# Output projection of an attention kernel: full-height products in one score bank, or pairs of 64-row products in the two banks of a pair

## The chip, the cores and the metric

One core of a Trainium2 chip runs the whole kernel. The metric is device time in microseconds (us) of one execution; lower is better. The granted TensorE clock was 0.999 of full speed over the profiled execution.

## The reference, cut to what matters

Two attentions over the same input are computed and mixed by a gate. `A` has 32 heads of 16, causal inside four blocks of 512 tokens, with a memory carried from block to block; `B` is a full attention over 2048 tokens. Each has its own output projection, and the change is in these two products and their sum.

```python
def _A_ref(x, wq, wk, wv, wo, beta):
    ...
    logits = jnp.einsum("bhqd,bhkd->bhqk", qs, ks) * scale + mask
    p = _softmax(logits, axis=-1)
    a_dot = jnp.einsum("bhqk,bhkd->bhqd", p, vs)
    ...
    o = g * a_mem + (1.0 - g) * a_dot
    ...
    return o @ wo

def _B_ref(x, wqkv, wo):
    ...
    o = jnp.einsum("bhqk,bhkd->bhqd", p, v)
    return (lambda x, *d: x.transpose(*d))(o, 0, 2, 1, 3).reshape(B, S, D) @ wo

g = _sigmoid((x * gate_w).sum(-1, keepdims=True))
return g * a + (1 - g) * b
```

The kernel puts the gate into the attention outputs, so that an output tile of 128 tokens is `oA @ woA + oB @ woB`, each with 512 inner elements and 512 columns.

## The kernel before, in words

**Units.** The attention is cut into 64 units: 32 of `A` (numbers 0 to 31) and 32 of `B` (32 to 63). A unit is four heads by 512 queries. After a stage of projections, the main loop runs `k` from 0 to 31 and does unit `32 + k` of `B` and unit `k` of `A` in 37 *groups*, numbered `n`. The instructions stand in the program in the order in which this loop writes them; nothing reorders them.

**A group** of `B` (`n` below 32) has, in this order:
- `t_group` (matmuls L528, exponentials on ScalarE L534): the transposed scores of two heads, as two products of 64 rows, one on the upper and one on the lower half of TensorE's rows. Each writes a bank of its own, out of the three banks `tb0`, `tb1` and `mb` (`misc` and `bank` hand out the one used longest ago). In the texts below this pair is T, with the group's number: T1 is that of group 1.
- the tasks that `plan` has for the group: nearly always one `s_b` (matmuls L474, reduction on VectorE L476), a pair of 64-row products for a later unit. It writes the two banks of one *pair of score banks*, `SBK[0]` or `SBK[1]` (`sbk` in the profile), handed out in turn by `rot`; VectorE then takes the row maxima over both banks. This pair is S below, and its reduction R.
- `pvs`: the products of exponentials and values (L550), four heads side by side in one bank, `pvb`. These are PV below. Group 1 has none.

The last five groups do the same for the `A` unit, with `s_a` (L452, L456, reductions L460 and L462) in place of `s_b`. `fin_copy` (L557) brings `pvb` out once per unit; the copy of the `A` unit falls into group 0 of the next `k`.

**The output slots.** From `k = 9` on, when four column blocks of heads are finished, one *slot* per `k` computes half of an output tile: slot `k - 9`, in group 1, by `out_mm(c, t, a)`. With `a = 0` it is the `A` half, with `a = 1` the `B` half of the same tile. `extras` puts it into `pre[1]`, behind the `s_b` of that group. The operands are split in a high and a low part: `AT["oh"]`, `AT["ol"]` hold the attention output of 128 tokens (made by `out_split` at the end of the unit before, on ScalarE L609 and GpSimd L610), `AT["wh"]`, `AT["wl"]` the weights. `TERMS` names three products (high by high, high by low, low by high), each over four blocks of 128 inner rows, so a slot is 12 products of 128 rows by 512 columns (L616), added up in one bank of the three. For `a = 0` ScalarE copies the bank to `yo` (L620); for `a = 1` VectorE adds it to `yo` (L623), and the SP queue sends the tile out (L624). At `k = 31` there is a second slot in group 28; what is left of the projection is done behind the loop.

VectorE, ScalarE and GpSimd each work through their instructions in program order, and so does the SP queue, which issues the transfers.

Of the kernel before, what the change touches and what calls it, by code (L numbers as in the profile page):

```python
# [7 lines left out]
FT = mybir.dt.float32  # L8
# [3 lines left out]
AF = mybir.ActivationFunctionType  # L12
OP = mybir.AluOpType
# [7 lines left out]
DM = 512  # L21
# [13 lines left out]
def gated_mix_kernel(ctx, tc, xt, wq, wk, wv, wo, beta, wqkv, wob, gate_w, out):  # L35
    nc = tc.nc
    outr = out.rearrange("b s d -> (b s) d")
# [47 lines left out]
    SBK = [PS.tile([128, 2, C], FT, name=f"sbk{i}") for i in range(2)]  # L85
# [23 lines left out]
    def rot(key, lst):  # L109
        i = cnt.get(key, 0)  # L110
        cnt[key] = i + 1
        return lst[i % len(lst)]
# [165 lines left out]
    TERMS = ((0, 0), (0, 1), (1, 0))  # L278
# [127 lines left out]
    def load_q(u):  # L406
        kd, qd, c = UN[u]
        load_qk(q_of(u), kd, 0, qd, c)

    def load_ka(u):  # L410
        kd, qd, c = UN[u]
        load_qk(KA[u % 2], kd, 1, qd, c)
# [67 lines left out]
    def m_chain(k):  # L480
        mx = pair_max(k)
        if k == 1:
            nc.vector.memset(mx[:, 0], 0.0)
        if k < 32:
            nc.vector.tensor_reduce(mx[:, 1], MXB.pop(32 + k).rearrange("q j p i c -> q (j p) i c"), axis=AX.X,
                                    op=OP.max)
        else:
            nc.vector.memset(mx[:, 1], 0.0)
        del MX[k]
        mx = mx.rearrange("q u h i -> q (u h i)")  # L490
        m8 = M8[k] = W.tile([128, 2, 32], FT, name="m8")
        hi = W.tile([128, 32], FR, name="mhi")
        nc.vector.tensor_scalar(hi, mx, -1.0, None, op0=OP.mult)
        nc.vector.tensor_copy(m8[:, 0], hi)
        nc.vector.scalar_tensor_tensor(m8[:, 1], mx, -1.0, hi, op0=OP.mult, op1=OP.subtract)
# [16 lines left out]
    AT = {}  # L512
# [3 lines left out]
    def t_group(u, n, banks):  # L516


        kd, qd, c = UN[u]
        bs = [bank(banks) for _ in range(2)]  # L520
        c0 = 0
        for it, hs in (((n // 2, (n % 2 * 2, n % 2 * 2 + 1)),) if kd == "B" else GA[n]):
            q0 = 128 * it if kd == "A" else 0
            w = C - q0
            pn = it if kd == "B" else it % 2
            for j, h in enumerate(hs):
                r = slice(64 * j, 64 * j + 64)
                nc.tensor.matmul(bs[j][:, c0:c0 + w], k_of(u, h // 2)[r, 128 * it:128 * it + 128],  # L528
                                 q_of(u)[r, h // 2, q0:], start=True, stop=True)
                PT[u, it, h] = PTILE[pn % 2][:, 2 + j if (kd, it) == ("A", 2) else h][:, c0:c0 + w]  # L530
            c0 += w
        for j in range(2):
            pt = PTILE[pn % 2][:, 2 + j if (kd, n) == ("A", 4) else hs[j]]
            nc.scalar.activation(pt, bs[j], AF.Exp, scale=SCALE)  # L534
            if kd == "A":
                m = pt[:, :128] if n < 2 else pt.rearrange("p (a t) -> p a t", a=4)[:, ::3 if n < 4 else 2]
                nc.gpsimd.affine_select(out=m, in_=m, pattern=[[1, 128]] if n < 2 else [[0, 2], [1, 128]],  # L537
                                        compare_op=OP.is_ge, fill=0.0, base=0, channel_multiplier=-1)
# [73 lines left out]
    def out_mm(c, t, a):  # L612
# [8 lines left out]
        else:  # L621
            tt = 4 * c + t
            nc.vector.tensor_tensor(AT["yo"], b, AT["yo"], op=OP.add)  # L623
            nc.sync.dma_start(outr[tt * 128:(tt + 1) * 128, :], AT["yo"])  # L624

    def tail_ops(t):
        s = KB[2 * (t // 2)][:, t % 2]
        return [s[:, 1024 * n:1024 * n + 1024].rearrange("p (g a t) -> p g a t", g=4, a=2) for n in range(2)]
# [29 lines left out]
    def todo(fn, *a):  # L658
        return lambda: fn(*a)
# [90 lines left out]
    for blk in range(16):  # L750
        g, c = divmod(blk, 4)
# [8 lines left out]
        n = blk + 1 + (c == 2)  # L760
# [74 lines left out]
    def late():  # L835
        proj.close()
        L = AT["L"] = ctx.enter_context(tc.tile_pool(name="late", bufs=1))
        VB[1] = L.tile([128, NT, 8, E + 1], FT, name="vb1")
        AT["o"] = [L.tile([128, 4, 2, C], FT, name=f"o{n}") for n in range(2)]
        AT["wh"] = L.tile([128, 4, 2, DM], FR, name="wh")  # L840
        AT["wl"] = L.tile([128, 4, 2, DM], FR, name="wl")
        AT["d"] = [L.tile([128, C], FT, name=f"d{n}") for n in range(2)]
        AT["oh"] = L.tile([128, 4, 2, 128], FR, name="oh")
        AT["ol"] = L.tile([128, 4, 2, 128], FR, name="ol")
        for p in range(2):
            set_aux(KB[2][:, p], 0)
# [6 lines left out]
    def pvs(k, n):  # L853

        ua, ub = k, 32 + k
        if n == 0:
            if k:
                pv(ua - 1, 2)
                fin_copy(ua - 1)
        elif k == 31 and n < 2 * NT:  # L860
            if n % 2 and n > 1:
                pv(ub, n // 2 - 1)
        elif 2 <= n < 2 * NT + 2:
            pv(ub, n // 2 - 1, n % 2 * 256, n % 2 * 256 + 256)
            if n == 2 * NT + 1:
                fin_copy(ub)
        elif n > 2 * NT + 1:
            m = n - 2 * NT - 2
            if m < 2:
                pv(ua, 0, 256 * m, 256 * m + 256)  # L870
            else:
                pv(ua, 1)
                pv(ua, 3)

    def extras(k):

        pre, post = {}, {}
        if not k:
            for n in range(4):
                pre[2 * n] = [fill[n - 4]]  # L880
        post[2 * S_LAST + 4] = [todo(m_rows, k + 1)]
        for n, at in [(k - 9, 1)] + [(23, 2 * OMI)] * (k == 31):
            if n >= 0:
                pre[at] = [todo(out_mm, n // 8, n // 2 % 4, n % 2)]
        return pre, post

    def beside(k, it):

        for f, it0, u in ((fin_load, NT + 1, 32 + k), (fin_rec, 5, 31 + k), (fin_bc, 6, 31 + k),
                          (fin_load, 1, k - 1), (fin_rec, 6, k - 1), (fin_bc, S_LAST + 2, k - 1)):  # L890
            if it == it0 and (k or it0 > NT):
                f(u)
        c, j = divmod(k - 1, 8)
        if k and j % 2:
            for kd, it0 in (("B", 9), ("A", 13)):
                if it == it0:
                    fin_norm(kd, j // 2, c)
        if k >= 8 and k % 2 == 0 and it == NT + 2:
            out_split(k // 8 - 1, k // 2 % 4)
        if (k, it) == (31, 4):  # L900
            grest = AT["grest"] = AT["o"][0][64:, 0, 0]
            nc.sync.dma_start(grest, GD[3 * C:].rearrange("(o t) -> o t", o=1).to_broadcast([64, C]))
        if (k, it) == (31, 9):
            grest = AT["grest"]
            nc.vector.tensor_scalar(grest, grest, nh[64:, 3:4], None, op0=OP.mult)
        if (k, it) == (31, NT + 2):
            fin_rec(63)
        if k == 31 and it == 13:
            o = AT["o"][1][:64, 3, 0]
            nc.gpsimd.tensor_tensor(o, o, AT["d"][0][:64], op=OP.mult)  # L910
        if k == 31 and it < 8 and it % 2 == 0:
            for a in range(2):
                tail_split(it // 2, slice(0, 3), a)


    ex = [extras(k) for k in range(32)]
    plan = {}

# [13 lines left out]
    for k in range(32):  # L932
        ua, ub = k, 32 + k
        banks = T3 + [b[:, 0] for b in SBK] * (k == 31)
        for n in range(NG):
            it = n // 2 if n < NG - 1 else NT + 2
            t_group(*(ub, n) if n < 2 * NT else (ua, n - 2 * NT), banks)
            for f in plan.get((k, n), []) + ex[k][0].get(n, []):
                f()
            pvs(k, n)  # L940
            for f in ex[k][1].get(n, []):
                f()
            if n % 2 == 0 and n < NG - 1:
                continue
            beside(k, it)
            if it == S_LAST:
                m_chain(k + 1)
            if it == 4 and not k:
                late()
            if it == 4 and not k:  # L950
                load_q(ub + 2)
                for c in range(NC4):
                    load_kb(2, c)
            if it == NT and k < 29:
                load_q(ub + 3)
                load_kb(k + 3)
            if it == 6 and k < 31:
                load_q(ua + 1)
                load_ka(ua + 1)
                if (ua + 1) % 2 == 0:  # L960
                    load_va(ua + 1)
            if it == 9:
                if k % 2 == 0 and k < 30:
                    load_vb(k // 2 + 1)
                if 1 <= k <= 4:
                    load_wo(k - 1)
# [55 lines left out]
```

## Time and profile before

| | |
|---|---|
| Median of 3 runs | 1960.63 us (1957.93 to 1960.81) |
| Profiled execution, its own time | 1956.4 us |
| Span, first to last instruction | 1954.7 us |
| Busy TensorE, VectorE, ScalarE, GpSimd | 1930.3, 1629.9, 1433.4, 275.8 us |
| Output slots in the loop | 24, each 12 matmuls of L616 |

A busy TensorE is counted from the start of a matmul to its modelled end, and matmuls overlap, so 99% says only that it seldom stood still. What a group costs is read from the starts of its rows. In a row of the timeline stand: start in us, duration in us, engine, line, operation, output and input tiles, shape, number of instructions merged into the row, and in brackets the idle time before it with what ended it. PE is TensorE, PEld its weight loads, DVE VectorE, ACT ScalarE, POOL GpSimd, SPq the SP queue.

### The profile page before, as it was taken

Reading aid. Unit: us, or ns where it says so; the run is one execution under the profiler, and the core shown is the slowest. Engines: PE = TensorE matmul, PEld = TensorE weight load, DVE = VectorE, ACT = ScalarE, POOL = GpSimd, SP = SyncE. Lnnn points to the kernel's source line nnn. Section 1 sums busy time; section 2 is a strip of 40 time slices with the busy share of each in tenths; the row PEclk is TensorE's granted clock in tenths of the full one; section 3 lists DMA queues with packets and bytes.
Section 4 is the critical chain, followed back from the end, with each engine's and each line's share of the span. In section 5 each row is a group of like instructions: output and inputs, shape, how many; then the busy total and the mean of one; then the engine's idle time right before and its main releaser. Section 6 shows DMA issues by size and latency. Waiting matters only on the chain.

```text
span 1954.7 us, 43539 instructions
## 1 busy us (share of the span) xinstructions
PE 1930.3 (99%) x17485; PEld 939.3 (48%) x17485; DVE 1629.9 (83%) x1798; ACT 1433.4 (73%) x2699; POOL 275.8 (14%) x497
## 2 busy tenths in 40 slices
PE   7999999999999999999999999999999999999999
PEld 5887777444344444444444444444444444444445
DVE  7135766899999999999999999999999999999942
ACT  4233333688888888888888888888888888888884
POOL 5201000012120101111111111111111111111022
PEclk9999999999999999999999999999999999999999
DMA  7666655644444444343435453444354444434111
GB/s 218 170 205 188 198 192 178 156 98 115 98 115 93 106 91 109 81 111 80 114 87 115 87 115 87 113 87 115 87 115 87 109 86 96 101 88 106 48 50 58
DMA packets 163790, 222.49 MB, mean 114 GB/s; under 512 B 39916, under 2 KB 90556, under 8 KB 157828
## 3 DMA queue, kind: packets, MB, share of 16 engines
q1 hardware_dynamic: 159284, 211.41, 43.7%
q0 software_dynamic: 3248, 8.03, 2.1%
q8 instruction: 138, 2.26, 0.5%
q14 instruction: 64, 0.52, 0.1%
q10 hardware_dynamic: 1056, 0.26, 0.1%
HBM read 147.95 MB, written 68.16 MB: 111 GB/s over the span
## 4 chain that ended last, share of the span: by engine, by line
PE 95%; DVE 3%; ACT 1%; SPq 1%; DMA 1%; issue 0%; DVEq 0%; ACTq 0%
PE pvb L550 33%; PE tb L528 17%; PE sbk L474 12%; PE mb L528 9%; PE tb L304 4%; PE sbk L452 3%; PE tb L616 2%; PE mb L304 2%; PE sbk L287 1%; DVE mxb L476 1%; PE tb L287 1%; PE pvb L304 1%; PE mb L616 1%; PE sbk L456 1%; PE mb L287 1%; PE pvb L287 1%
## 5 line engine op out<-in xcount | busy, mean ns | idle before, releaser
L476 DVE TENSOR_REDUCE mxb<-sbk 128x2 f32<-128x1024 f32 x1024 | 1222.3, 1222 | 67.3 <-PE sbk L474 63.1
L534 ACT ACTIVATE raw<-tb 128x512 f32<-128x512 f32 x1555 | 887.5, 598 | 152.9 <-PE tb L528 89.6
L550 PE MATMUL pvb<-raw,vb 128*17 128x256 f32 (+1 forms) x8072 | 639.3, 388 | 0.0
L534 ACT ACTIVATE raw<-mb 128x512 f32<-128x512 f32 x782 | 467.6, 598 | 79.5 <-PE tb L528 44.8
L528 PE MATMUL tb<-qb,xh 64*128 64x512 f32 x872 | 331.6, 495 | 1.7 <-ACT raw L534 1.7
L550 PEld LDWEIGHTS pvb<-raw,vb 128*17 128x17 f32 x8072 | 134.4, 95 | 340.1 <-issue 336.6
L474 PE MATMUL sbk<-xh,qb 64*128 64x512 f32 x1344 | 281.5, 395 | 2.7 <-DVE mxb L476 1.8
L528 PE MATMUL mb<-qb,xh 64*128 64x512 f32 x445 | 220.6, 496 | 0.0
L537 POOL TENSOR_SCALAR_AFFINE_SELECT raw<-raw 128x256 f32<-128x256 f32 (+1 forms) x320 | 115.5, 361 | 709.6 <-ACT raw L534 701.7
L528 PEld LDWEIGHTS tb<-qb,xh 64*128 64x128 f32 x872 | 124.7, 183 | 179.6 <-issue 89.9
L528 PE MATMUL tb<-qb,kb 64*128 64x512 f32 x470 | 179.5, 496 | 1.3 <-DVE st L314 0.8
L460 DVE TENSOR_REDUCE mx<-sbk 128x2 f32<-128x768 f32 (+1 forms) x128 | 136.7, 1090 | 22.9 <-PE sbk L456 18.3
L474 PE MATMUL sbk<-kb,qb 64*128 64x512 f32 x704 | 146.4, 398 | 0.0
L474 PEld LDWEIGHTS sbk<-xh,qb 64*128 64x128 f32 x1344 | 138.3, 186 | 7.4 <-DVE mxb L476 5.0
L528 PEld LDWEIGHTS mb<-qb,xh 64*128 64x128 f32 x445 | 81.3, 183 | 95.2 <-issue 50.4
L590 POOL TENSOR_TENSOR o<-o,d 128x512 f32<-128x512 f32 x31 | 39.7, 1281 | 545.6 <-DMA d<-rd 461.9
L528 PEld LDWEIGHTS tb<-qb,kb 64*128 64x128 f32 x470 | 68.2, 183 | 100.1 <-issue 52.6
L528 PE MATMUL mb<-qb,kb 64*128 64x512 f32 x234 | 116.1, 496 | 0.0
L550 PE MATMUL pvb<-raw,va 128*17 128x256 f32 (+2 forms) x1280 | 94.7, 384 | 0.8 <-ACT pvs L559 0.8
L452 PE MATMUL sbk<-ka,qa 64*128 64x256 f32 (+3 forms) x512 | 88.2, 358 | 1.1
L528 PE MATMUL tb<-qa,ka 64*128 64x512 f32 (+3 forms) x339 | 79.5, 372 | 0.0
L311 ACT ACTIVATE st<-tb 128x512 fp32r<-128x512 f32 x33 | 19.8, 599 | 80.2 <-DVE phi L310 40.5
(284 smaller groups left out, 1837.6 us busy)
## 6 DMA issues: line engine op xcount, KB each, us to landing
xh<-dB SPq DMA_DIRECT2D x38, 512.0 KB
vb<-vdB SPq DMA_DIRECT2D x16, 1088.0 KB
dB<-st SPq DMA_DIRECT2D x64, 256.0 KB
dA<-st SPq DMA_DIRECT2D x64, 256.0 KB
pd<-pvs SPq DMA_DIRECT2D x64, 256.0 KB
kb<-dB SPq DMA_DIRECT2D x22, 512.0 KB
xh<-dB SPq DMA_DIRECT2D x38, 256.0 KB
qb<-dB SPq DMA_DIRECT2D x64, 128.0 KB
```

The source lines that it names most:

```text
L287: nc.tensor.matmul(b, lhs, WV[wi][:, k, :], start=n == 0, stop=n == 11)
L304: nc.tensor.matmul(b, WS[ws][w][wi][:, k, :], (XH, XL)[xi][c][:, k, :], start=n == 0, stop=n == 11)
L452: nc.tensor.matmul(b[:, j, c0:c0 + n], q_of(u)[r, p, i * 128:(i + 1) * 128], k_of(u, p)[r, :n], start=True, stop=False)
L460: nc.vector.tensor_reduce(m[:, :, p, i], b[:, :, :n], axis=AX.X, op=OP.max)
L474: nc.tensor.matmul(b[:, j], q_of(u)[r, p, i * 128:(i + 1) * 128], k_of(u, p)[r, kc * C:(kc + 1) * C], start=True, stop=True)
L476: nc.vector.tensor_reduce(MXB[u][:, :, p, i, kc], b, axis=AX.X, op=OP.max)
L528: nc.tensor.matmul(bs[j][:, c0:c0 + w], k_of(u, h // 2)[r, 128 * it:128 * it + 128], q_of(u)[r, h // 2, q0:], start=True, stop=True)
L534: nc.scalar.activation(pt, bs[j], AF.Exp, scale=SCALE)
L537: nc.gpsimd.affine_select(out=m, in_=m, pattern=[[1, 128]] if n < 2 else [[0, 2], [1, 128]], compare_op=OP.is_ge, fill=0.0, base=0, channe ...
L550: nc.tensor.matmul(PVB[32 * h:32 * h + E + 1, q0 + lo:q0 + hi], vt[:, it, 4 * q + h, :], pt[:, lo:hi], start=it == 0 and lo == 0, stop=it ...
L590: nc.gpsimd.tensor_tensor(o, o, d, op=OP.mult)
L616: nc.tensor.matmul(b, (AT["oh"], AT["ol"])[oi][:, g, a], (AT["wh"], AT["wl"])[wi][:, g, a], start=n == 0, stop=n == 11)
```

## The change

For the slots at `k = 9` to 30 (22 of the 24) `out_mm` is replaced by `out_rows`. It takes a pair of score banks by `rot`, as `s_b` does, and splits each 128-row product into two of 64 rows: the upper rows add up in the pair's first bank, the lower rows in its second. The two partial sums then have to be added, and the two halves of the tile too. For `a = 0` VectorE copies the second bank (`yp`) and ScalarE the first (`yo`). For `a = 1` VectorE adds the second bank to `yp`, ScalarE copies the first to `yq`, and GpSimd adds `yq` and then `yp` to `yo`, which goes out as before.

The place changes too. The slot now stands ahead of the `s_b` of group 1, and at these `k` the `s_b` of group 2 moves to group 3, which so has two.

```diff
+    def out_rows(c, t, a):
+        b = rot("s", SBK)
+        for n, (oi, wi, g) in enumerate([(oi, wi, g) for oi, wi in TERMS for g in range(4)]):
+            for j in range(2):
+                r = slice(64 * j, 64 * j + 64)
+                nc.tensor.matmul(b[:, j], (AT["oh"], AT["ol"])[oi][r, g, a], (AT["wh"], AT["wl"])[wi][r, g, a],
+                                 start=n == 0, stop=n == 11)
+        if a == 0:
+            AT["y"] = [AT["L"].tile([128, DM], FT, name=n) for n in ("yo", "yp")]
+            nc.vector.tensor_copy(AT["y"][1], b[:, 1])
+            nc.scalar.activation(AT["y"][0], b[:, 0], AF.Copy)
+        else:
+            tt = 4 * c + t
+            y0, y1 = AT["y"]
+            y2 = AT["L"].tile([128, DM], FT, name="yq")
+            nc.vector.tensor_tensor(y1, b[:, 1], y1, op=OP.add)
+            nc.scalar.activation(y2, b[:, 0], AF.Copy)
+            nc.gpsimd.tensor_tensor(y0, y0, y2, op=OP.add)
+            nc.gpsimd.tensor_tensor(y0, y0, y1, op=OP.add)
+            nc.sync.dma_start(outr[tt * 128:(tt + 1) * 128, :], y0)
...
-                pre[at] = [todo(out_mm, n // 8, n // 2 % 4, n % 2)]
+                pre[at] = [todo(out_rows if k < 31 else out_mm, n // 8, n // 2 % 4, n % 2)]
...
-            for f in plan.get((k, n), []) + ex[k][0].get(n, []):
+            tasks = plan.get((k, n), [])
+            if 9 <= k < 31 and n in (2, 3):
+                tasks = plan[k, 2] + plan[k, 3] if n == 3 else []
+            own = ex[k][0].get(n, [])
+            for f in own + tasks if k else tasks + own:
                 f()
```

TensorE's rows of `k = 9` from the T of group 1 to the T of group 3, before (`sbk_114` and `sbk_115` are the two pairs of score banks; L528 is T, L474 is S, L550 is PV, L616 the slot):

```order
L528 MATMUL tb_110<-qb_70,kb_89 128x512
L528 MATMUL mb<-qb_70,kb_89 128x512
L474 MATMUL sbk_115<-xh_87,qb_68 128x512 x2
L616 MATMUL tb_111<-wh,oh 128x512 x4
L616 MATMUL tb_111<-wl,oh 128x512 x4
L616 MATMUL tb_111<-wh,ol 128x512 x4
L528 MATMUL tb_110<-qb_70,kb_89 128x512
L528 MATMUL mb<-qb_70,kb_89 128x512
L474 MATMUL sbk_114<-xh_87,qb_68 128x512 x2
L550 MATMUL pvb<-raw_86,vb_75 17x256 x4
L528 MATMUL tb_111<-qb_70,kb_89 128x512
L528 MATMUL tb_110<-qb_70,kb_89 128x512
```

The same place now, up to the PV of group 3 (L631 is the slot):

```order
L631 MATMUL sbk_115<-wh,oh 128x512 x8
L631 MATMUL sbk_115<-wl,oh 128x512 x8
L631 MATMUL sbk_115<-wh,ol 128x512 x8
L474 MATMUL sbk_114<-xh_87,qb_68 128x512 x2
L528 MATMUL tb_111<-qb_70,kb_89 128x512
L528 MATMUL tb_110<-qb_70,kb_89 128x512
L550 MATMUL pvb<-raw_86,vb_75 17x256 x4
L528 MATMUL mb<-qb_70,kb_89 128x512
L528 MATMUL tb_111<-qb_70,kb_89 128x512
L474 MATMUL sbk_115<-xh_87,qb_68 128x512 x2
L474 MATMUL sbk_114<-xh_87,qb_68 128x512 x2
```

The slot went from a bank of the three to a pair of score banks and stands ahead of the S that used to precede it; two S stand behind one another in group 3. Over the three groups the pairs of T and S and the PV products are the same ones.

VectorE's rows at that place now (L557 copies `pvb`, L635 is the slot's copy; before, the second L476 stood where L635 stands, and no row lay between it and the third):

```order
L476 TENSOR_REDUCE mxb<-sbk_114 128x2
L557 COPY pvs<-pvb 128x512
L635 COPY yp<-sbk_115 128x512
L476 TENSOR_REDUCE mxb<-sbk_114 128x2
L476 TENSOR_REDUCE mxb<-sbk_115 128x2
```

The reduction of group 1's S now stands behind the slot's copy (or, for `a = 1`, the slot's add L641), where before it stood ahead of anything that the slot has for VectorE.

## The prediction

> **What bounds the kernel now.** I read the page first, then the timeline of single slots on TensorE (PE) and VectorE (DVE), then the places where one waits for the other. On the page, the busy times and the chain that ended last:
>
> ```profile
> PE 1930.3 (99%) x17485; PEld 939.3 (48%) x17485; DVE 1629.9 (83%) x1798; ACT 1433.4 (73%) x2699; POOL 275.8 (14%) x497
> ...
> PE 95%; DVE 3%; ACT 1%; SPq 1%; DMA 1%; issue 0%; DVEq 0%; ACTq 0%
> ```
>
> The chain runs along TensorE, so what counts is when TensorE starts each group. What a slot costs is seen from one copy of `pvb` to the next (L557, VectorE, once per `k`), in one `k` without a slot and the first `k` with one:
>
> ```profile
> 687.34 0.68 DVE L557 COPY pvs<-pvb 128x512 f32<-128x512 f32 x1
> 734.99 0.68 DVE L557 COPY pvs<-pvb 128x512 f32<-128x512 f32 x1
> ...
> 782.98 0.68 DVE L557 COPY pvs<-pvb 128x512 f32<-128x512 f32 x1
> 833.24 0.68 DVE L557 COPY pvs<-pvb 128x512 f32<-128x512 f32 x1
> ```
>
> 47.65 us without and 50.26 us with a slot: a slot costs about 2.6 us, all told some 60 us in the loop. In a slot with `a = 1`, T1, S1, the twelve products, then T2, S2 and so on:
>
> ```profile
> 832.54 0.50 PE L528 MATMUL mb<-qb,xh 64*128 64x512 f32 x1
> 832.88 0.40 PE L474 MATMUL sbk<-xh,qb 64*128 64x512 f32 x2
> 833.13 0.60 ACT L534 ACTIVATE raw<-mb 128x512 f32<-128x512 f32 x1 [0.20 <-PE mb L528]
> 833.20 1.19 PE L616 MATMUL tb<-wh,oh 128*128 128x512 f32 x4
> 833.63 0.59 ACT L534 ACTIVATE raw<-tb 128x512 f32<-128x512 f32 x1
> 833.84 1.22 DVE L476 TENSOR_REDUCE mxb<-sbk 128x2 f32<-128x1024 f32 x1
> 834.23 1.07 PE L616 MATMUL tb<-wl,oh 128*128 128x512 f32 x4
> 835.14 1.07 PE L616 MATMUL tb<-wh,ol 128*128 128x512 f32 x4
> 836.14 0.50 PE L528 MATMUL mb<-qb,xh 64*128 64x512 f32 x1
> 836.31 0.69 DVE L623 TENSOR_TENSOR yo<-tb,yo 128x512 f32<-128x512 f32 x1 [1.26 <-PE tb L616]
> 836.92 1.22 DVE L476 TENSOR_REDUCE mxb<-sbk 128x2 f32<-128x1024 f32 x1
> ...
> 838.57 0.50 PE L528 MATMUL tb<-qb,xh 64*128 64x512 f32 x2
> ```
>
> The starts give the price list. From T1 to T4 it is 838.57 - 832.54 = 6.03 us. The twelve products take 2.94 of it (833.20 to 836.14); the middle four take 0.91, or 0.2275 each. R1, the reduction of S1, runs at 833.84 beside the products. That is the point for all that follows: S1 is already out when the slot begins, so VectorE has it to reduce meanwhile. A slot with `a = 0`:
>
> ```profile
> 782.28 0.50 PE L528 MATMUL tb<-qb,kb 64*128 64x512 f32 x1
> 782.46 0.49 PE L528 MATMUL mb<-qb,kb 64*128 64x512 f32 x1
> 783.58 1.22 DVE L476 TENSOR_REDUCE mxb<-sbk 128x2 f32<-128x1024 f32 x1
> 786.41 0.39 PE L474 MATMUL sbk<-xh,qb 64*128 64x512 f32 x2
> 786.85 12.28 DVE L476 TENSOR_REDUCE mxb<-sbk 128x2 f32<-128x1024 f32 x10 [2.05 <-PE sbk L474]
> 788.53 0.49 PE L528 MATMUL mb<-qb,kb 64*128 64x512 f32 x1
> ```
>
> T1 to T4 is 788.53 - 782.28 = 6.25 us; the second half of T1 comes 0.18 late (782.46). An ordinary group, T4 to T5:
>
> ```profile
> 788.53 0.18 PEld L528 LDWEIGHTS mb<-qb,kb 64*128 64x128 f32 x1 [0.42 <-ACT raw L534]
> 788.64 0.19 PEld L474 LDWEIGHTS sbk<-xh,qb 64*128 64x128 f32 x2
> 788.87 0.40 PE L474 MATMUL sbk<-xh,qb 64*128 64x512 f32 x2
> 789.19 0.63 PE L550 MATMUL pvb<-raw,vb 128*17 128x256 f32 x8
> 789.75 0.50 PE L528 MATMUL tb<-qb,kb 64*128 64x512 f32 x1
> ```
>
> T takes 0.34 after a PV, S before a PV 0.32, PV 0.56: 1.22 us. Where no PV stands between, as in group 1 without a slot, S to T:
>
> ```profile
> 447.64 0.40 PE L474 MATMUL sbk<-kb,qb 64*128 64x512 f32 x2
> 447.88 0.39 PE L528 MATMUL tb<-qb,xh 64*128 64x512 f32 x1
> ...
> 686.97 0.40 PE L474 MATMUL sbk<-xh,qb 64*128 64x512 f32 x2
> 687.20 0.39 PE L528 MATMUL tb<-qb,xh 64*128 64x512 f32 x1
> ```
>
> 0.24 and 0.23 for a pair of 64-row products behind another pair. So a pair behind PV pays 0.10 for its exposed weight load and the change of shape, and one ahead of PV 0.08.
>
> **The change part by part.** Removed are 12 products at 0.2275, with the two changes between full and half height around them. Added are 24 products as 12 pairs. The trace of before has no row of twelve pairs in one go. The nearest are the two above; I take 0.237 a pair. Bounds: 0.2275, the full-height product, which streams as many columns, and 0.24. So 12 x 0.237 = 2.84 us, which saves 0.10 of the 2.94. The pairs' own weight loads I count at nothing: S loads its weights from 788.64 to 788.83, under T's matmuls (788.53, 0.49 long), on the same two halves of the rows. If that cover went, 0.19 a pair would show. Here "TensorE: Matmul & The Clock Gate" of the Trainium skill, Part 3 (The mechanism), speaks against the change: weight loads overlap with matmuls in flight only where the row groups differ, and pair after pair uses the same two. The row above disagrees with it; its price is a rival below.
>
> The new order, counted from T1. The first pair follows T1 after 0.34, as S1 did (0.34 + 0.18 = 0.52 with `a = 0`, where the second half is late). The slot ends, and S1 starts, at E = 0.34 + 2.84 = 3.18 (`a = 1`) or 3.36 (`a = 0`). From E on TensorE alone would need S1 0.24, T2 0.32, PV 0.56, T3 0.34, S2 0.24, and would be at S3 at E + 1.70. S3 writes the banks that S1 wrote, so it waits for R1, and R1 is now behind the slot's copy or add on VectorE. What that takes, with the rows for the hand-over:
>
> ```profile
> 825.77 1.23 DVE L460 TENSOR_REDUCE mx<-sbk 128x2 f32<-128x1024 f32 x1
> 827.05 0.19 PEld L452 LDWEIGHTS sbk<-ka,qa 64*128 64x128 f32 x2 [0.15 <-DVE mx L460]
> ```
>
> From the end of a stream to VectorE's start 0.20 (S at 786.41, its 0.24, and 786.85); the add 0.61 until the next can start (836.31 to 836.92), the copy 0.60 (782.98 to 783.58); R1 1.22; from its end (827.00) to the weight load 0.05. Sum 2.08 or 2.07: S3 starts at E + 2.08, a new wait of 0.38 us. Queued behind S3 is everything on TensorE: PV3, T4, S4. As S3 starts from a stop, its load is bare: 0.32 + 0.10 = 0.42 to PV3, and 0.56 to T4. So T4 is at E + 3.06 (3.05): 6.24 after T1 instead of 6.03, and 6.41 instead of 6.25. That is +0.21 and +0.16 us. If the semaphore held back only the matmul and not the load, each would be 0.10 less.
>
> One more wait comes behind. With ScalarE's copy of the slot first (from E + 0.20, next start 0.50 later, by 833.13 to 833.63), T2's first exponential ends at E + 1.30 and frees the bank for T3's second half at E + 1.35, where T3 starts at E + 1.12. S2 then ends at E + 1.46 + 0.23 + 0.24 = E + 1.93, R2 runs from E + 2.13 to 3.35, and the load of S4, which would be hidden at T4 + 0.11 = E + 3.17, comes at 3.40: S4 starts 0.10 late. Slot by slot then +0.31 and +0.26 us. Bounds for this term: nothing, or a second 0.10 at S5, if that load is late too.
>
> Off the path, with their cover:
>
> ```profile
> 802.11 6.87 DVE L476 TENSOR_REDUCE mxb<-sbk 128x2 f32<-128x1024 f32 x6
> 809.16 2.45 DVE L476 TENSOR_REDUCE mxb<-sbk 128x2 f32<-128x1024 f32 x2 [0.17 <-PE sbk L474]
> ...
> L590 POOL TENSOR_TENSOR o<-o,d 128x512 f32<-128x512 f32 x31 | 39.7, 1281 | 545.6 <-DMA d<-rd 461.9
> ...
> 837.03 0.36 SPq L624 DMA_DIRECT2D out_dram<-yo  x1
> 845.01 0.53 SPq L567 DMA_DIRECT2D o<-pd  x1
> ```
>
> VectorE is later than before by R1 and, with `a = 0`, the copy; but six reductions in 6.87 us start every (6.87 - 1.22) / 5 = 1.13 us, TensorE asks for one in 1.22, and at 809.16 VectorE stands idle. It catches up about 0.09 a group, over some ten groups; only if it did not would the lag reach TensorE. GpSimd's two adds, 11 x 2 x 1.28 us, lie in its idle time (545.6 us before L590 alone) and make the output's transfer about 2.6 us later; the next one on SP stands 8 us behind (845.01), so nothing there waits.
>
> Sum: 11 slots of each kind, 11 x (0.31 + 0.26) = +6.3 us. Against the profiled execution (1956.4 us, the span and 1.7 around it) that gives 1962.7; that execution lies 4.2 under the median of the runs shown, so the forecast for the median is 1960.63 + 6.3 = 1966.9 us. Its own range: with 0.2275 a pair (-0.11), hidden load at S3 (-0.10) and no wait at S4 (-0.10) the slots stand at 0.00 and -0.05, -0.6 us; with 0.24 (+0.04) and the second wait (+0.10) at +0.45 and +0.40, +9.4 us. So 1960.0 to 1970.0.
>
> **The rivals.** *The wait at S3 is hidden: faster.* Without it and what follows from it, T1 to T4 is 6.24 - 0.38 - 0.10 = 5.76 and 6.41 - 0.37 - 0.10 = 5.94, so -0.27 and -0.31 a slot, 11 x -0.58 = -6.4 us: 1954.2. It decides at the point where R1 ends before TensorE is through with S2, 0.38 us earlier than I have it. For it: VectorE is idle 2.05 us in the slot of before, and TensorE drops two changes of shape. Against it: the order puts R1 behind the copy, and copy and reduction are both measured.
>
> *VectorE sets the pace afterwards: much slower.* If the reductions started only every 1.22 us, VectorE would keep its lag. R2 started 4.38 us after T1 before (836.92) and starts at 3.18 + 2.13 = 5.31 now; with `a = 0` 4.57 and 5.49. That is 0.92 a slot, 20 us: 1981. The six reductions in 6.87 us speak against it.
>
> *The pairs do not stream.* If each half had to finish its matmul before its next weights load, a pair would take 0.24 + 0.19 = 0.43, the twelve 5.16 instead of 2.84, and 22 slots 51 us more: 2018. This is also what the rule of the Trainium skill quoted above would make of it; the change would then not run side by side what it splits. The weight load at 788.64 speaks against it.
>
> **How the numbers follow.** About 0.2%, 3.9 us, is what a measurement of this kernel can tell from no change. Forecast 0.70: about three quarters of its range (+3.9 to +9.4 and the likeliest value) counts as slower, 0.52, and 0.18 as the same. Hidden wait 0.16, faster. VectorE's pace 0.09 and pairs that do not stream 0.05, slower. So faster 0.16, same 0.18, slower 0.66. The range takes in the forecast's own and the hidden wait, and a little above for a wait that is longer than worked out: 1954.0 to 1972.0; it leaves out 0.14.
>
> **What the profile of the changed kernel would show.** The first L631 row 0.34 us behind T1, and 2.7 to 2.9 us from it to S1; the weight load of S3, the second L474 of group 3, with an idle time of 0.3 to 0.5 us put down to DVE; T4 6.2 to 6.4 us behind T1; from one copy of `pvb` to the next 50.5 to 50.6 us instead of 50.26. Wrong would be: no wait at S3 and 50.0 us (the first rival), waits of L474 for DVE over many groups (the second), or over 4 us from the first L631 to S1 (the third).

## The result and the profile after

The changed kernel takes 1980.63 us (median of 5 runs, 1979.66 to 1981.17) against 1958.12 (5 runs): a ratio of 1.011, 95% interval 1.0095 to 1.0124, 22.5 us slower. Slower was forecast, but +6.3 us and a range that ended at 1972.0: the direction was right, the size was not. Most of the difference is a wait that the prediction did not have.

The page of the changed kernel, busy times and chain:

```profile
PE 1940.2 (98%) x17749; PEld 958.7 (48%) x17749; DVE 1626.2 (82%) x1809; ACT 1436.3 (73%) x2710; POOL 304.6 (15%) x519
...
PE 92%; DVE 5%; ACT 2%; DMA 1%; issue 1%; SPq 0%; DVEq 0%; ACTq 0%
```

TensorE's share of the chain fell from 95% to 92%, and VectorE's and ScalarE's rose from 3% and 1% to 5% and 2%: TensorE now waits for them. Where, the copies of `pvb` show. Of the changed kernel, the first three from the first slot on, and the window from the second to the last, of before (first row) and after (second row), with the busy times of the engines:

```profile
785.18 0.68 DVE L557 COPY pvs<-pvb 128x512 f32<-128x512 f32 x1
836.46 0.68 DVE L557 COPY pvs<-pvb 128x512 f32<-128x512 f32 x1
887.64 0.68 DVE L557 COPY pvs<-pvb 128x512 f32<-128x512 f32 x1
...
833.24:1884.80 1051.56, 1050.83 (x10558) 447.52 (x10556) 960.79 (x986) 869.13 (x1616) 142.28 (x254) 1.00 0.42 96
...
836.46:1909.20 1072.74, 1059.47 (x10810) 465.02 (x10806) 956.02 (x996) 872.17 (x1627) 170.72 (x276) 1.00 0.41 94
```

Over 21 periods the window is 50.07 us before and 51.08 after: 1.01 us a slot, and 22 slots make 22.2 us. The loss is in the slots. A slot with `a = 1`, to be held against the one at 832.54 of before; then the T5 of before, which the prediction did not need:

```profile
835.76 0.50 PE L528 MATMUL tb<-qb,xh 64*128 64x512 f32 x1
836.09 1.09 PE L631 MATMUL sbk<-wh,oh 64*128 64x512 f32 x8
837.00 1.10 PE L631 MATMUL sbk<-wl,oh 64*128 64x512 f32 x8
838.82 0.44 PE L474 MATMUL sbk<-xh,qb 64*128 64x512 f32 x2
839.07 0.69 DVE L641 TENSOR_TENSOR yp<-sbk,yp 128x512 f32<-128x512 f32 x1 [1.93 <-PE sbk L631]
839.79 0.60 ACT L642 ACTIVATE yq<-sbk 128x512 f32<-128x512 f32 x1 [2.36 <-DVE yp L641]
839.98 0.49 PE L528 MATMUL mb<-qb,xh 64*128 64x512 f32 x1
840.29 1.08 ACT L534 ACTIVATE raw<-tb 128x512 f32<-128x512 f32 x2
840.93 0.49 PE L528 MATMUL tb<-qb,xh 64*128 64x512 f32 x1 [0.46 <-ACT raw L534]
840.94 0.95 PE L474 MATMUL sbk<-xh,qb 64*128 64x512 f32 x4
841.70 4.62 DVE L476 TENSOR_REDUCE mxb<-sbk 128x2 f32<-128x1024 f32 x4 [0.81 <-PE sbk L474]
842.38 0.50 PE L528 MATMUL tb<-qb,xh 64*128 64x512 f32 x1
842.98 0.49 PE L474 MATMUL sbk<-xh,qb 64*128 64x512 f32 x2
843.96 0.51 PE L528 MATMUL tb<-qb,xh 64*128 64x512 f32 x2
...
839.79 0.49 PE L528 MATMUL mb<-qb,xh 64*128 64x512 f32 x1
```

T1 to T5 was 839.79 - 832.54 = 7.25 us and is 843.96 - 835.76 = 8.20. The row to look at is ScalarE's copy at 839.79. The slot ends at 838.82, yet the copy starts 0.97 later, and the bracket says what it waited for: not TensorE but VectorE's add of the *other* bank, which ends at 839.76. T2's exponentials stand behind it (840.29), the second half of T3 waits for the bank of the first of them (840.93, where the first half was at 839.98), and S2 and S3 follow only then. VectorE stands idle for 0.81 us, R2 starts at 841.70, and S4, which needs the banks of R2, comes 0.60 behind T4 instead of 0.34. The waits over all slots:

```profile
ACT yo L636 <- DVE yp L635: 28.5, 11, 2.6
ACT yq L642 <- DVE yp L641: 25.9, 11, 2.4
PE tb L528 <- ACT raw L534: 10.8, 22, 0.5
PEld sbk L474 <- DVE mxb L476: 9.3, 22, 0.4
```

Every slot has it: 11 and 11 copies of ScalarE behind VectorE, 22 late halves of T3, 22 late S4.

### The profile page after: what moved, and what is told of

Read it like the earlier page. It is cut to its first block, busy times and chain, and to the rows that moved or that the text cites. A ratio compares the mean times of both kernels' runs of the same rounds, so it can differ in the third digit from the quotient of the medians.

```text
span 1979.4 us, 44120 instructions
## 1 busy us (share of the span) xinstructions
PE 1940.2 (98%) x17749; PEld 958.7 (48%) x17749; DVE 1626.2 (82%) x1809; ACT 1436.3 (73%) x2710; POOL 304.6 (15%) x519
## 4 chain that ended last, share of the span: by engine, by line
PE 92%; DVE 5%; ACT 2%; DMA 1%; issue 1%; SPq 0%; DVEq 0%; ACTq 0%
PE pvb L550 31%; PE tb L528 17%; PE sbk L474 12%; PE mb L528 9%; PE tb L304 5%; PE sbk L631 3%; PE sbk L452 3%; DVE mxb L476 3%; PE mb L304 2%; PE sbk L287 1%; PE tb L287 1%; PE pvb L304 1%; PE sbk L456 1%; PE mb L287 1%; PE pvb L287 1%; ACT raw L534 1%
## 5 line engine op out<-in xcount | busy, mean ns | idle before, releaser
L476 DVE TENSOR_REDUCE mxb<-sbk 128x2 f32<-128x1024 f32 x1024 | 1209.5, 1221 | 64.3 <-PE sbk L474 60.8
L550 PE MATMUL pvb<-raw,vb 128*17 128x256 f32 (+1 forms) x8072 | 639.4, 388 | 0.0
L528 PE MATMUL tb<-qb,xh 64*128 64x512 f32 x865 | 330.9, 492 | 8.6 <-ACT raw L534 8.6
L550 PEld LDWEIGHTS pvb<-raw,vb 128*17 128x17 f32 x8072 | 134.5, 95 | 336.6 <-issue 333.2
L474 PE MATMUL sbk<-xh,qb 64*128 64x512 f32 x1344 | 286.0, 399 | 5.3 <-DMA xh<-dB 1.9
L528 PE MATMUL mb<-qb,xh 64*128 64x512 f32 x452 | 223.8, 495 | 0.0
L528 PEld LDWEIGHTS tb<-qb,xh 64*128 64x128 f32 x865 | 125.0, 183 | 185.8 <-ACT raw L534 94.2
L528 PE MATMUL tb<-qb,kb 64*128 64x512 f32 x462 | 176.8, 492 | 5.3 <-ACT raw L534 4.5
L474 PE MATMUL sbk<-kb,qb 64*128 64x512 f32 x704 | 148.1, 401 | 0.8
L474 PEld LDWEIGHTS sbk<-xh,qb 64*128 64x128 f32 x1344 | 139.8, 186 | 15.4 <-DVE mxb L476 10.9
L528 PEld LDWEIGHTS mb<-qb,xh 64*128 64x128 f32 x452 | 82.6, 183 | 95.7 <-issue 52.3
L528 PE MATMUL mb<-qb,kb 64*128 64x512 f32 x242 | 120.1, 496 | 0.0
L528 PEld LDWEIGHTS tb<-qb,kb 64*128 64x128 f32 x462 | 66.8, 183 | 98.4 <-ACT raw L534 48.2
L550 PE MATMUL pvb<-raw,va 128*17 128x256 f32 (+2 forms) x1280 | 94.9, 384 | 1.1 <-ACT pvs L559 1.1
L528 PE MATMUL tb<-qa,ka 64*128 64x256 f32 (+3 forms) x347 | 79.0, 375 | 0.0
```

What stands on the lines that cost most here:

```text
L474: nc.tensor.matmul(b[:, j], q_of(u)[r, p, i * 128:(i + 1) * 128], k_of(u, p)[r, kc * C:(kc + 1) * C], start=True, stop=True)
L476: nc.vector.tensor_reduce(MXB[u][:, :, p, i, kc], b, axis=AX.X, op=OP.max)
L550: nc.tensor.matmul(PVB[32 * h:32 * h + E + 1, q0 + lo:q0 + hi], vt[:, it, 4 * q + h, :], pt[:, lo:hi], start=it == 0 and lo == 0, stop=it ...
```

## The experiments

**Theory W:** ScalarE's copy waits for VectorE's, because both banks are one tile for the program, and all that follows comes from this. **Rival R:** the new order, which puts R1 behind the slot's copy. **Rival P:** the pairs themselves or GpSimd's adds. All comparisons are with runs of before on the same chip; "slot part" is the time from the copy of `pvb` in the first slot to the last one in the profile, 1101.8 us before (782.98 to 1884.8) and 1124.0 after (785.18 to 1909.2), so +22.2. It comes from one profiled execution of each version. Up to the first slot all versions run the same program, and there these executions already lie 6 us apart (782.98 to 788.87), so two or three us of slot part are not to be read alone.

**ScalarE reads elsewhere.**

```diff
-            nc.scalar.activation(AT["y"][0], b[:, 0], AF.Copy)
+            nc.scalar.activation(AT["y"][0], AT["wl"][:, 0, 0], AF.Copy)
...
-            nc.scalar.activation(y2, b[:, 0], AF.Copy)
+            nc.scalar.activation(y2, AT["wl"][:, 0, 1], AF.Copy)
```

> ScalarE copies a tile of weights in place of the slot's first bank, so it no longer reads the pair of score banks; the sum of the upper 64 rows is left out of the result. Size and number of all instructions are as in the changed kernel. Theory W (ScalarE's copy waits for VectorE's copy of the other bank, its exponentials come late, and the second half of T3 waits for its bank): the wait of T3 goes, only the wait of S3 for R1 is left, 0.05 to 0.15 us a slot over before, 1959 to 1962 us. Rival R (R1 behind the slot's copy is the main cost): about 1979 us. Rival P (the pairs or GpSimd's adds slow something else): about 1980 us.

1961.66 us, ratio 1.0014 (1.0005 to 1.0024), slot part +3.0. Of the timeline, the slot with `a = 1` (the slot's end and S1 are at 837.48):

```profile
835.98 0.63 ACT L642 ACTIVATE yq<-wl 128x512 f32<-128x512 f32 x1
838.14 1.09 ACT L534 ACTIVATE raw<-tb 128x512 f32<-128x512 f32 x2 [1.53 <-PE tb L528]
838.33 6.98 DVE L476 TENSOR_REDUCE mxb<-sbk 128x2 f32<-128x1024 f32 x6
838.79 0.49 PE L528 MATMUL tb<-qb,xh 64*128 64x512 f32 x1
838.98 1.12 PE L474 MATMUL sbk<-xh,qb 64*128 64x512 f32 x4
839.60 0.19 PEld L474 LDWEIGHTS sbk<-xh,qb 64*128 64x128 f32 x2 [0.52 <-DVE mxb L476]
840.59 0.50 PE L528 MATMUL tb<-qb,xh 64*128 64x512 f32 x1
```

The copy has gone ahead of the slot's end, the exponentials follow T2 at once, T4 is 3.11 us behind the slot's end instead of 3.56. Nineteen of the 22 us are gone, with the order, the pairs, R1's place and GpSimd's adds unchanged. R and P are refuted as the main cause. The wait that the prediction did have is here: the weight load of S3 (839.60) stands 2.12 us behind the slot's end and is put down to VectorE. One thing differs besides the wait: ScalarE's copy needs nothing of the slot here and runs ahead of its end. The last two experiments keep it behind.

**ScalarE first, VectorE second.**

```diff
-            nc.vector.tensor_copy(AT["y"][1], b[:, 1])
             nc.scalar.activation(AT["y"][0], b[:, 0], AF.Copy)
+            nc.vector.tensor_copy(AT["y"][1], b[:, 1])
...
-            nc.vector.tensor_tensor(y1, b[:, 1], y1, op=OP.add)
             nc.scalar.activation(y2, b[:, 0], AF.Copy)
+            nc.vector.tensor_tensor(y1, b[:, 1], y1, op=OP.add)
```

> The two readers change places in the program: ScalarE copies the first bank, then VectorE the second. W together with the wait of S3: the second half of T3 is in time (about 1.35 us after the slot's end E), but VectorE starts 0.65 us later, R1 ends at E + 2.7, S3 starts there and T4 at E + 3.7, about as measured in the changed kernel (E + 3.6): 1980 to 1985 us. W alone, R1 without weight: about 1965 us. R alone: 22 x 0.65 us more than the changed kernel, 1995 us. P: 1980 us.

1977.24 us, ratio 1.0091 (1.0076 to 1.0106), slot part +17.6; a little less than expected, with T4 3.73 us behind the slot's end, where 3.7 had been worked out. The wait has turned round, and with it the loss:

```profile
DVE yp L642 <- ACT yq L641: 28.2, 11, 2.6
...
840.79 0.69 DVE L642 TENSOR_TENSOR yp<-sbk,yp 128x512 f32<-128x512 f32 x1 [2.56 <-ACT yq L641]
...
842.67 0.49 PE L474 MATMUL sbk<-xh,qb 64*128 64x512 f32 x2 [0.64 <-DVE mxb L476]
```

Whoever is second in the program waits. Now R1 is behind two readers, and S3 waits 0.64 us for it.

**The old place, with the pairs.**

```diff
-            tasks = plan.get((k, n), [])
-            if 9 <= k < 31 and n in (2, 3):
-                tasks = plan[k, 2] + plan[k, 3] if n == 3 else []
-            own = ex[k][0].get(n, [])
-            for f in own + tasks if k else tasks + own:
+            for f in plan.get((k, n), []) + ex[k][0].get(n, []):
```

> Pairs, banks and adds as in the changed kernel, but in the old place: S1 ahead of the slot, S2 in its own group. W: R1 runs beside the slot again, but ScalarE still waits for VectorE's copy, the second half of T3 comes at E + 2.1 and T4 at E + 3.3; with E at T1 + 3.32 that is 0.6 us a slot over before, 1971 us. R: the cost was the place, 1953 to 1959 us. P: 1980 us.

1979.07 us, ratio 1.0104 (1.0084 to 1.0124), slot part +20.1: 8 us above what I worked out for W, and far from R. Of its slot and its waits:

```profile
840.81 0.60 ACT L642 ACTIVATE yq<-sbk 128x512 f32<-128x512 f32 x1 [2.98 <-DVE yp L641]
...
841.95 0.49 PE L528 MATMUL tb<-qb,xh 64*128 64x512 f32 x1 [0.46 <-ACT raw L534]
...
PEld sbk L631 <- DVE mxb L476: 10.0, 22, 0.5
```

The second reader's wait is as in the changed kernel. New is that the slot itself waits for R0, as its pair is the one that S0 wrote; I had left that 0.25 us out. Starting from that stop, the twelve pairs also take 2.86 us instead of 2.73 (1.04 for the first four, 0.91 for the others), so the slot ends 3.70 us after T1 and not 3.32: 22 times 0.38 are the 8 us. P's 1980 us is near too, but the first experiment, with the same pairs and adds, leaves P no such cost.

**The new order without the pairs.**

```diff
-                pre[at] = [todo(out_rows if k < 31 else out_mm, n // 8, n // 2 % 4, n % 2)]
+                pre[at] = [todo(out_mm, n // 8, n // 2 % 4, n % 2)]
```

> The new order alone: the twelve full-height products in one of the three banks as before, but ahead of S1, and S2 moved to group 3. W: R1 comes late by the add (a = 1) or the exponentials by the copy (a = 0), 0.2 to 0.3 us a slot, 1962 to 1965 us. R: most of the loss is here, 1975 us or more. P: 1958 us, nothing of it.

1975.11 us, ratio 1.0082 (1.0063 to 1.01), slot part +13.1. I had expected 4 to 6 us; 1975 is what R had named. In the slot with `a = 1` (839.00 its T1) the slot waits for its bank at the start, and the two S after R1 and R2 wait:

```profile
839.45 0.76 PEld L616 LDWEIGHTS tb<-wh,oh 128*128 128x128 f32 x4 [0.27 <-ACT raw L534]
...
844.46 0.19 PEld L474 LDWEIGHTS sbk<-xh,qb 64*128 64x128 f32 x2 [0.34 <-DVE mxb L476]
...
845.87 0.19 PEld L474 LDWEIGHTS sbk<-xh,qb 64*128 64x128 f32 x2 [0.24 <-DVE mxb L476]
```

So the new order is no gift. With full-height products in one of the three banks, the slot starts 0.45 us after T1, as ScalarE's exponentials free the bank late, and ends 3.41 after it; the changed kernel has 0.33 and 3.06. R1 and R2 are then late enough to be waited for twice. T5 comes 7.86 us after T1 here, 7.25 before; by my estimate about 0.55 of these 0.61 us are the two waits: S3 follows S2 after 0.49 instead of 0.24 and T4 follows S3's load after 0.99 instead of 0.88 (its load is bare), and T5 follows T4 after 1.41 instead of 1.22. Order and pairs both lose alone, by 13 and (in the old place) 20 us, and 22 together; the losses do not add up. With pairs and without the wait for a second reader the same order costs 3 us (first experiment), so what R names is mostly a cost of the full-height products in that place, and not of the changed kernel.

The next three stay in the old place and vary who reads the pair; the fourth goes back to the new place.

**Old place, ScalarE first**: the edits of the second and the third experiment together.

> Pairs in the old place (S1 ahead of the slot, S2 in its own group), and ScalarE reads its bank first, VectorE second. Against the third experiment only the order of the two readers differs. W: ScalarE is on time, the second half of T3 is 0.2 us late at most, S1's reduction runs beside the products; what is left is the slot's wait of 0.25 us for R0 and a late R2: -0.1 to +0.2 us a slot against before, 1957 to 1962 us. If the old place itself were the cost there (the slot's wait for R0), it would stay near 1979 us.

1963.05 us, ratio 1.0019 (1.001 to 1.0028), slot part +4.6, a microsecond above the range. Against the third experiment (+20.1) only the order of the two readers differs. Here R1 runs beside the products, so VectorE can afford to be second.

**Old place, VectorE alone.** The lines that empty the pair, in place of the two copies and the adds:

```diff
+            nc.vector.tensor_reduce(AT["y"], b.rearrange("p j c -> p c j"), axis=AX.X, op=OP.add)
...
+            nc.vector.tensor_reduce(y1, b.rearrange("p j c -> p c j"), axis=AX.X, op=OP.add)
+            nc.gpsimd.tensor_tensor(AT["y"], AT["y"], y1, op=OP.add)
```

> Pairs in the old place, and one reduction on VectorE adds the two banks (1024 elements in, about 1.22 us, read with a stride of a bank), so that ScalarE has no part in the slot; GpSimd adds the two halves of the tile. W: no wait at T3, S3 waits at most 0.1 us for the bank, T4 at E + 2.45: 0 us a slot against before with a = 1 and -0.2 us with a = 0, 1954 to 1959 us. Rival: a sum read with a stride is slower than a row maximum, or VectorE then sets the pace (46.8 + 0.5 to 1.2 us of work in a period of 50): 1963 us or more.

1960.39 us, ratio 1.0005 (0.9994 to 1.0016), slot part +1.8: no difference from before, though 1.4 us above the range. The sum of the two banks (`a = 1`), and S3 that waits for it (`a = 0`):

```profile
839.18 1.23 DVE L639 TENSOR_REDUCE yp<-sbk 128x512 f32<-128x1024 f32 x1 [1.42 <-PE sbk L631]
...
790.20 0.19 PEld L474 LDWEIGHTS sbk<-xh,qb 64*128 64x128 f32 x2 [0.25 <-DVE yo L635]
```

The sum costs 1.23 us, as a row maximum over as many elements. VectorE takes it without setting the pace.

**Old place, ScalarE alone.** Again the lines that empty the pair:

```diff
+            nc.scalar.activation(AT["y"], b, AF.Copy)
...
+            nc.scalar.activation(y1, b, AF.Copy)
+            nc.gpsimd.tensor_tensor(y, y, y1, op=OP.add)
+            nc.gpsimd.tensor_tensor(y[:, 0], y[:, 0], y[:, 1], op=OP.add)
```

> Pairs in the old place, and ScalarE copies both banks in one instruction (about 1.06 us), so that VectorE has no part in the slot and nobody waits for a second reader; GpSimd adds. W: the wait is gone, but ScalarE's exponentials for T2 start 0.46 us later than behind a copy of one bank, and the second half of T3 comes at E + 1.8: about 0.3 us a slot over before with a = 1, less with a = 0, 1961 to 1967 us, between the sixth and the third experiment. Rival: what costs is that two engines read the pair, whatever their order: 1957 us or less.

1974.13 us, ratio 1.0071 (1.0057 to 1.0084), slot part +12.9; twice what I expected (the "sixth experiment" of the text above is the old place with ScalarE first).

```profile
841.44 1.02 ACT L640 ACTIVATE yp<-sbk 128x1024 f32<-128x1024 f32 x1 [2.21 <-PE sbk L631]
...
843.00 0.49 PE L528 MATMUL tb<-qb,xh 64*128 64x512 f32 x1 [0.16 <-ACT raw L534]
843.01 0.72 PE L474 MATMUL sbk<-xh,qb 64*128 64x512 f32 x2
```

Nobody waits for a second reader here, but ScalarE is late by the longer copy, and T3's second half with it. In the old place the slot ends 3.70 us after T1 in this version, in the third experiment and with ScalarE first; T3's second half comes 1.80, 2.10 and 1.37 behind that, and the slot part is +12.9, +20.1 and +4.6. So the cost goes with how late T2's exponentials start, whatever makes them late.

**The changed kernel without the move of S2.**

```diff
             tasks = plan.get((k, n), [])
-            if 9 <= k < 31 and n in (2, 3):
-                tasks = plan[k, 2] + plan[k, 3] if n == 3 else []
```

> The changed kernel without the move of S2: the slot is ahead of S1, but S2 stays in group 2. S2 needs the pair that the slot wrote, and gets it when ScalarE, behind VectorE, has read it, at E + 1.75 instead of E + 0.5; T3 then no longer has to wait. W: T4 at E + 3.85 against E + 3.6 in the changed kernel, 1982 to 1987 us. R: with one S less waiting for R1 in group 3 it gets faster, 1970 us.

1978.05 us, ratio 1.0092 (1.0079 to 1.0106), slot part +19.3: 3 us less than with the move (the intervals just overlap), where I had expected more. S2 now takes the wait in place of T3; S4 is no longer late, and T5 follows T4 after 1.22 us as before the change:

```profile
841.67 0.49 PE L474 MATMUL sbk<-xh,qb 64*128 64x512 f32 x2 [0.95 <-ACT yq L642]
```

**Two tiles.** The two halves go to banks of different tiles, with nothing left out.

```diff
         b = rot("s", SBK)
+        m = misc()
...
-                nc.tensor.matmul(b[:, j], ...
+                nc.tensor.matmul(m if j == 0 else b[:, 1], ...
```

ScalarE reads `m`, VectorE `b[:, 1]`; first in the new place, then in the old one.

> The changed kernel with nothing left out, but the upper rows' products add up in one of the three banks (ScalarE reads that) and the lower rows' in the second bank of a pair of score banks (VectorE reads that): the two readers have no tile in common. W: ScalarE waits for TensorE alone, the second half of T3 is about 0.2 us late, and what is left is S3 behind R1, as in the first experiment with ScalarE's copy back in its place: 3 to 8 us over before, 1962 to 1967 us. Rival: the two halves in unlike banks do not run side by side, or a third user of the three banks holds T2 up: 1975 us or more.

> The same two tiles in the old place, S1 ahead of the slot. W: neither a second reader nor R1 behind the slot; left are the slot's wait for R0 (0.25 us) and the second half of T3 0.2 us late, against 0.1 to 0.2 us saved in the products: 0 to +4 us against before, 1958 to 1963 us. Rival: the place matters by itself, as in the fourth experiment, and takes off more than R1's wait: 1955 us or less.

New place: 1967.18 us, ratio 1.0044 (1.0031 to 1.0058), slot part +8.8, at the upper end of what was expected. Old place: 1956.69 us, ratio 0.9989 (0.9979 to 0.9999), slot part -2.1 (784.26 to 1884.0), a little below the range. Of the old place, `a = 1`, from the slot's end:

```profile
837.39 0.60 ACT L643 ACTIVATE yq<-tb 128x512 f32<-128x512 f32 x1 [2.02 <-PE tb L632]
...
837.61 0.69 DVE L642 TENSOR_TENSOR yp<-sbk,yp 128x512 f32<-128x512 f32 x1 [1.40 <-PE mb L528]
...
838.53 0.49 PE L528 MATMUL tb<-qb,xh 64*128 64x512 f32 x1
838.53 0.49 PE L528 MATMUL mb<-qb,xh 64*128 64x512 f32 x1
...
839.75 0.50 PE L528 MATMUL tb<-qb,xh 64*128 64x512 f32 x2
```

ScalarE now waits for TensorE alone, both readers run at the same time, and both halves of T3 are on time. The full computation with the pairs loses its wait when the halves are two tiles, which settles W: the slot part falls by 13.4 us in the new place and by 22.2 in the old one (+20.1 to -2.1). What is left in the new place has two parts. With `a = 1`, T4 comes 3.10 us behind the slot's end, as in the first experiment (3.11), with S3 behind R1. But the upper rows now need one of the three banks, and the slot starts 0.45 instead of 0.33 us after T1 and ends 3.29 after it instead of 3.06; with `a = 0` it ends 3.53 after it instead of 3.21. Eleven slots of each make 6 us of that, about the difference from the +3.0 of the first experiment. In the old place it is the one version that is measured faster than both kernels, by 0.1%, with an interval that just leaves out no change; as one of ten versions it is no more than a hint.

## Why the prediction was right or wrong

- *Direction, and that the place of the loss is between the slot's end and T4*: right, but in good part by luck. The wait that the forecast rests on makes about 3 of the 22 us (first experiment).
- *The pairs, 0.237 us each*: 837.00 - 836.09 = 0.91 for four, 0.2275 each, the lower bound. The slot ended 3.06 us after T1, not 3.18. With `a = 0` they took 2.86 in all, 0.238 each, near the forecast, and the slot ended 3.20 after T1, not 3.36. The rival that pairs do not stream fell: 24 weight loads of 0.18 us each had no time of their own here. The sentence of the Trainium skill ("TensorE: Matmul & The Clock Gate", Part 3, The mechanism) that weight loads overlap only between row groups does not hold in these rows; the same section also names a background weight buffer as a way to load early, which would fit them, though no run here shows it.
- *S3 waits 0.38 us for R1*: hidden in the changed kernel, as S2 and S3 both stood behind the late half of T3. In the first experiment, without that, it was there: S3's load came 2.12 behind the slot's end, where 2.08 was forecast, T4 3.11, where 3.06 was, and the kernel at +2.4 us by the medians (1961.66 against 1959.24).
- *The step that failed*: "with ScalarE's copy of the slot first (from E + 0.20 ...)". E is the slot's end. It started at E + 0.97. I took the two readers to run side by side, because they read different banks. In the trace of the changed kernel L636 and L642 wait for a semaphore of VectorE alone and for none of TensorE; with the two halves in two tiles ScalarE waits for TensorE. So T3's second half came not at E + 1.35 but at E + 2.11, and T4 at E + 3.56.
- *S4 0.10 us late*: the mechanism was there, but S4 started 0.26 late, and with its bare load T5 came 1.58 behind T4 instead of 1.22, so 0.36. The reason is the same late T3, through S2 and R2.
- *Rivals*: the hidden wait did not occur. VectorE did not set the pace either: its four reductions from 841.70 take 4.62 us, so 1.13 each from start to start, as estimated. That this rival's 1981 us lies next to the measured time is chance.
- *GpSimd and the output's transfer at no cost*: the first experiment has both and is 2.4 us from before, which leaves them little.

Three of my sums in the experiments were off too. In the third, and with ScalarE alone, T3's second half came behind the slot's end as worked out (2.10 and 1.80 us), but the slot itself ended late. In the new order alone I had left out the slot's wait for its bank and the wait of S4. Behind a slot, one late step makes two or three others late, and a sum of single waits comes out too small.

## What to carry to other kernels

Before costing two engines that empty two banks side by side, look in the program at what each waits for: if the banks belong to one tile, the second reader waits for the first, and where that engine also frees the banks of the tensor engine, the delay reaches it in full (here a copy 0.77 us later than forecast, and 0.87 us a slot gone with the wait in the first experiment). A product moved to another buffer should be priced with the engine that empties it and with everything queued on that engine. And an engine that would stand idle in the slot is better given its work ahead of the slot than behind it: with ScalarE as first reader the slot part is +4.6 with S1 ahead of the slot and +17.6 with S1 behind it.

## What the runs showed of the hardware

With `a = 1`, the twelve pairs of 64-row products of the changed kernel take 2.73 us (836.09 to 838.82), 0.2275 a pair, the pace of full-height products with as many columns (0.91 for four in either kernel); the twelve full-height products of before took 2.94 with their changes of shape. With `a = 0` the pairs take 2.86:

```profile
784.82 1.26 PE L631 MATMUL sbk<-wh,oh 64*128 64x512 f32 x8
787.68 0.48 PE L474 MATMUL sbk<-xh,qb 64*128 64x512 f32 x2
```

In the third experiment, where they start from a stop, they take 2.86 too. So splitting the rows saved 0.08 to 0.2 us in these slots; why the `a = 0` slots run slower than 0.2275 a pair stays open. VectorE adds two banks read with a stride of a bank in 1.23 us for 1024 elements, the same as a row maximum over contiguous ones.
